# A gated linear attention with a feed-forward block on one core: another written order for its steps, and a normalising weight folded into a centring

## The chip, the core and the metric

The kernel runs on one core of a Trainium2 chip. A core has a matrix engine (TensorE, "PE" in the profile, with its weight loads as "PEld"), a vector engine (VectorE, "DVE"), a scalar engine for functions of one argument (ScalarE, "ACT"), a general engine (GpSimd, "POOL") and queues for transfers between the memory of the chip and the core (mostly SyncE, "SP"). Each engine takes its own instructions in order; engines wait for each other through semaphores. Matrix products land in PSUM, a small memory that VectorE and ScalarE read. The metric is the time of one execution in microseconds of device time.

## The reference

Two blocks, one behind the other. The first is a recurrence with complex decays over 768 positions, for 4 batches of 8 heads of width 48:

```python
mag = np.sqrt(a_re * a_re + a_im * a_im)
scale = np.minimum(mag, 0.999) / (mag + 1e-06)
a_re_n, a_im_n = (a_re * scale, a_im * scale)
for t in range(S):
    S_re, S_im = a_re_n * S_re - a_im_n * S_im + k_t v_t^T, a_re_n * S_im + a_im_n * S_re
    y[:, :, t] = einsum('bhd,bhde->bhe', q[:, :, t], S_re)
```

(The loop is shortened here: the decays act on the rows of the state.) Its output, 3072 rows of 384, enters the second:

```python
h = x @ w_in                                   # 384 -> 1024
sm = softmax(h)
solu = h * sm
ln = (solu - solu.mean()) / np.sqrt(solu.var() + 1e-06) * g_ln
return ln @ w_out                              # 1024 -> 384
```

The weights w_in, w_out and g_ln come to the kernel as float64 for the two matrices, and are converted on the core.

## The kernel before

There are N = 24 **chunks**: 6 stretches of 128 positions, each for 4 batches. Two chunks (two batches of a stretch) form a **group**; there are 12 groups. The function `whole` holds the fast path; `general` is a fallback that runs only if a flag says so, and is not touched.

**Preparation of a group** (`prep_steps`, L648 to L756). It turns the decays of both chunks into running logarithms of magnitude (f_lr) and running phases (f_x, then f_f), in small steps: s0 (clip on VectorE, then a logarithm and an inverse on ScalarE), s1 (four VectorE passes to the tangent of the half angle; the last two become a step of their own by the change), square, s2 and fourth (ScalarE), s3 and s4 (magnitude), totals (L691: a product with a triangular matrix on TensorE that sums the logarithms, then a VectorE clamp that writes f_lr), angle (L725: arctangent on ScalarE, then a VectorE pass that adds what the previous stretch handed on, f_on), phases (L733: a product on TensorE, f_phase, then ScalarE and VectorE passes), trig (L746: sine and cosine into f_cs), decay (L698: two exponentials), decayed (L706: k and q multiplied by them, one call for each chunk), ends (L711: the decay of the whole chunk, turned by a small TensorE transpose, f_tot). The arctangent and the sine need another table set on ScalarE than exponential and logarithm; to_trig and to_exp load one, and each pair of chunks needs both.

**Then a chunk.** doubled (L764) multiplies k and q by cosine and sine into f_k2 and f_q2 (the profile calls them f_k and f_q, with L768), turn (L775) transposes them on TensorE in four calls (k and q, two halves each) and ScalarE copies each result out of PSUM. score (L790) multiplies them in two halves and VectorE applies the causal mask (f_att), values (L802) forms the output of the chunk from f_att and the carried state, VectorE copies it out (f_xn), and carry (L818) updates the state (f_d, f_state).

**Then the feed-forward block of that chunk** (`ffn_steps`, L835): turn_x (f_xt, f_xT), up (L847, f_h) and solu (L854: exponential on ScalarE, product on VectorE, f_z) in two halves, turn_z (L861, f_zt, f_zT) in two halves, norm (L870: statistics on VectorE, two tiny GpSimd instructions, f_rs), down (L888, f_o) in two halves, and store (L895: scaled copy f_ot on VectorE, then the transfer to the output).

The order is written out by hand for TensorE, VectorE and ScalarE: each executes in the order in which `whole` calls the steps. The steps of three stages are laid side by side in the loop over n (L989 on): chunk n goes through score, values and carry; chunk n-1 through turn_x, up, solu, turn_z and norm; chunk n-2 through down, and n-3 through store. In an even step n the group after (`now`) goes from s1 to phases; in an odd one through trig, decay, decayed and ends, while `then`, the group behind it, does s0. Chunk n+1 is doubled and turned during step n.

The tiles sit in rings of few buffers, and a step waits until the reader of the buffer's previous user is through. The ring ps_t in PSUM has two places, which f_xt, f_turned, f_L, f_phase, f_zt and f_tot use in the order in which they are called; f_o has one place, f_score and f_h two each. The raw weights (f_raw) have six places for fourteen tiles (six of w_in, eight of w_out); fetch transfers one tile, raised (ScalarE) and convert (VectorE) turn it into float32. They are transferred a second time from step 4 on, only to be looked at by inspect.

Before the loop stands the **head**: the preparation of group 0, woven with the conversion of w_in. Steps n = 0 and 1 of the loop also convert w_out: for each of its eight tiles raised (ScalarE), convert (VectorE), scale (L634, ScalarE: w_out times g_ln); after n = 1's come centre (L637: a product with ones gives the column means, then eight VectorE passes subtract them).

Of the kernel before, what the change touches and what calls it, by code (L numbers as in the profile page):

```python
# [10 lines left out]
FP = mybir.dt.float32  # L11
# [3 lines left out]
AF = mybir.ActivationFunctionType  # L15
# [3 lines left out]
P = 128  # L19
# [497 lines left out]
def whole(ctx, tc, flag, q, k, v, a_re, a_im, moe_w_in, moe_w_out, moe_g_ln, out):  # L517
# [76 lines left out]
    def weight_steps():  # L594


        NW = 512
        steps = []
        for w, src, nk in ((w_in, moe_w_in, KD), (w_out, moe_w_out, KF)):
            wide = src.bitcast(I32).rearrange("(c p) w -> p c w", p=P)  # L600
            nf = w.shape[2]
            for f0 in range(0, nf, NW):
                for c in range(nk):
                    steps.append((w, wide, c, f0, min(NW, nf - f0)))

        def fetch(i):
            w, wide, c, f0, n = steps[i]
            raw = rawp.tile([P, NW, 2], I32, tag="raw", name="f_raw")[:, 0:n]
            nc.sync.dma_start(out=raw.rearrange("p n u -> p (n u)"), in_=wide[:, c, 2 * f0:2 * (f0 + n)])
            T["raw", i] = raw  # L610

        def raised(i):

            w, wide, c, f0, n = steps[i]
            y = T["bits", i] = bits.tile([P, NW], I32, tag="bits", name="f_bits")[:, 0:n]
            nc.scalar.activation(out=y.bitcast(FP), in_=T["raw", i][:, :, 0].bitcast(U32), func=AF.Identity,
                                 scale=2.0 ** -29, bias=magic)
            nc.scalar.activation(out=y, in_=y.bitcast(FP), func=AF.Identity, bias=mmagic)

        def convert(i):  # L620
            w, wide, c, f0, n = steps[i]
            hi, x = T["raw", i][:, :, 1], w[:, c, f0:f0 + n].bitcast(I32)

            nc.vector.tensor_scalar(out=x, in0=hi, scalar1=3, scalar2=0x3FFFFFFF, op0=OP.logical_shift_left,
                                    op1=OP.bitwise_and)
            nc.vector.scalar_tensor_tensor(out=x, in0=hi, scalar=-2 ** 30, in1=x, op0=OP.bitwise_and,
                                           op1=OP.bitwise_or)
            nc.vector.tensor_tensor(out=x, in0=x, in1=T["bits", i], op=OP.add)

        def inspect(i):  # L630
            nc.vector.tensor_reduce(out=least[:, i:i + 1], in_=T["raw", i][:, :, 1].bitcast(FP), axis=AX.X, op=OP.min,
                                    apply_absolute_value=True)

        def scale(c):  # L634
            nc.scalar.activation(out=w_out[:, c], in_=w_out[:, c], func=AF.Copy, scale=g_ln[:, c:c + 1])

        def centre():  # L637
            ps = ps_o.tile([P, DM], FP, tag="o", padded_shape=[P, 512], name="f_mean")
            for c in range(KF):
                nc.tensor.matmul(out=ps, lhsT=ones, rhs=w_out[:, c], start=(c == 0), stop=(c == KF - 1))  # L640
            for c in range(KF):
# [3 lines left out]
        return fetch, raised, convert, inspect, scale, centre  # L645


    def prep_steps(g):  # L648
# [3 lines left out]
        def s0():  # L652
            for nm in ("lr", "x0", "u"):
# [5 lines left out]
            nc.scalar.activation(out=lr, in_=ar, func=AF.Ln)  # L659
            nc.scalar.activation(out=x0, in_=lr, func=AF.Exp, scale=-1.0)  # L660
            nc.vector.tensor_scalar(out=ai, in0=ai, scalar1=1e15, scalar2=-1e15, op0=OP.min, op1=OP.max)

        def s1():

            ar, ai, x0 = st["ar"], st["ai"], st["x0"]
            nc.vector.tensor_tensor(out=ai, in0=ai, in1=x0, op=OP.mult)
            nc.vector.tensor_tensor(out=x0, in0=ar, in1=x0, op=OP.mult)
            nc.vector.scalar_tensor_tensor(out=x0, in0=x0, scalar=2.0, in1=ai, op0=OP.subtract, op1=OP.mult)
            nc.vector.tensor_scalar(out=x0, in0=x0, scalar1=1.5, scalar2=-1.5, op0=OP.min, op1=OP.max)  # L669

# [40 lines left out]
        def ends():  # L711
# [6 lines left out]
            e2 = sml.tile([GH, 2, D], FP, tag="e2", name="f_e2")  # L718
            nc.vector.tensor_copy(out=e2, in_=e.unsqueeze(1).to_broadcast([GH, 2, D]))
            ps = ps_t.tile([P, GH], FP, tag="t", padded_shape=[P, 512], name="f_tot")  # L720
            nc.tensor.transpose(out=ps[0:D2], in_=e2.rearrange("p u d -> p (u d)"), identity=ident[0:GH, 0:GH])
            tot = T["tot", g] = sml.tile([D2, GH], FP, tag="tot", name="f_tot")
# [2 lines left out]
        def angle():  # L725
            x0 = st["x0"]
            nc.scalar.activation(out=x0, in_=x0, func=AF.Arctan)  # L727
            if ti > 0:

                nc.vector.scalar_tensor_tensor(out=x0[0:1], in0=T["on", g - B // GB], scalar=2.0 * math.pi,  # L730
                                               in1=x0[0:1], op0=OP.mult, op1=OP.add)
# [14 lines left out]
        def trig():  # L746
# [8 lines left out]
        return dict(s0=s0, s1=s1, square=square, s2=s2, fourth=fourth, s3=s3, s4=s4, totals=totals, decay=decay,  # L755
                    decayed=decayed, ends=ends, angle=angle, phases=phases, trig=trig)  # L756

    def to_trig():
        nc.scalar.preload_act_table_set("trig_and_small")
# [180 lines left out]
    nc.vector.memset(magic, MAGIC)  # L940
    nc.vector.memset(mmagic, -MAGIC)
    nc.vector.memset(seen, 0.0)
    fetch, raised, convert, inspect, scale, centre = weight_steps()
    fetch(0)
    fetch(1)
    load(0, ("k", "q"))
# [6 lines left out]
    prep = [prep_steps(g) for g in range(NG)]  # L953
    first = prep[0]
    first["s0"]()
    to_trig()
    first["s1"]()
    raised(0)
    first["square"]()
    first["angle"]()  # L960
    convert(0)
    to_exp()
    first["s2"]()
    raised(1)
    first["s3"]()
    first["phases"]()
    convert(1)
    first["s4"]()
    first["totals"]()
    raised(2)  # L970
    convert(2)
    first["fourth"]()
    first["decay"]()
    to_trig()
    first["trig"]()
    to_exp()
    first["decayed"](0)
# [6 lines left out]
    raised(3)  # L984
    convert(3)
    prep[1]["s0"]()

    last = {}
    for n in range(N + 2):  # L989
# [8 lines left out]
        turn_x, up, solu, turn_z, norm = last[n - 1][:5] if n - 1 in range(N) else 5 * (None,)  # L998
# [7 lines left out]
        if n == 0:  # L1006
            for i in range(6, 14):
                fetch(i)
        if 4 <= n < 18:
            fetch(n - 4)  # L1010

        if n - 3 in range(N):
            last.pop(n - 3)[6]()
        if turn_x:
            turn_x()
        if n < N:
            score(0)
            score(1)
        if now and not odd:
            now["s1"]()  # L1020
        if now and odd:
            now["trig"]()
            to_exp()
            now["decay"]()
        if down:
            down(0)
        if nxt and not odd:
            doubled(nxt)
        if n == 0:
            raised(4)  # L1030
            convert(4)
        if n < N:
            values()
        if now and not odd:
            now["square"]()
        if up:
            up(0)
            solu(0)
        if now and not odd:
            now["s2"]()  # L1040
        if now and odd:
            now["decayed"](0)
        if nxt and odd:
            doubled(nxt)
        if now and odd:
            now["decayed"](1)
        if nxt:
            turn("k", nxt, 0)
            turn("q", nxt, 0)
        if n == 0:  # L1050
            raised(5)
            convert(5)
        if up:
            up(1)
            solu(1)
        if now and not odd:
            now["s3"]()
        if now and odd:
            now["ends"]()
# [5 lines left out]
        if n in (0, 1):  # L1065
            for i in range(6 + 4 * n, 10 + 4 * n):
                raised(i)
                convert(i)
                scale(i - 6)
        if n == 1:  # L1070
            centre()
        if now and not odd:
            now["s4"]()
        if then and odd:
            then["s0"]()
        if up:
            turn_z(0)
        if now and not odd:
            now["totals"]()
            now["fourth"]()  # L1080
            to_trig()
            now["angle"]()
        if down:
            down(1)
        if up:
            turn_z(1)
            norm()
        if 4 <= n < 18:
            inspect(n - 4)
        if n == N:  # L1090
            verdict()
        if now and not odd:
            now["phases"]()
    last.pop(N - 1)[6]()


@with_exitstack
# [54 lines left out]
```

## Time and profile before

| What | Value |
|---|---|
| Median of three runs | 688.5 us (687.51 to 689.68) |
| The profiled execution | 690.01 us |
| Its span, first to last instruction | 688.1 us |
| Mean granted clock of TensorE | 0.896 of full speed |
| Transfers | 42.23 MB, mean 61 GB/s |

The page also gives the span in 40 slices of 17.2 us, in tenths of busy time:

```profile
PE   1162776878878878878878878878878888789995
...
PEclk9975775999999999988999999999997999899999
DMA  8978150203214214214214203203203000000000
```

The first seven slices are the head with n = 0 and 1; TensorE is little used there, its granted clock (PEclk) is low in several of them, and the transfers are dense until the fourth. From there to slice 36 stand the pairs of steps. Time of the profile is that of one execution, and its rows are given as start and length in microseconds from the first instruction; in brackets stands how long the engine was idle before, and what released it.

### The profile page before, as it was taken

The page shows a single profiled execution, that of the slowest core. Times are in us where ns is not written, and L with a number is a line of the kernel's source. Part 1 is how long each engine was busy: PE and PEld are TensorE (multiplying, and loading weights), DVE is VectorE, ACT ScalarE, POOL GpSimd, SP SyncE. Part 2 cuts the span into 40 slices and gives each one's busy share as a digit, 9 for nine tenths or more (in the row PEclk, how much of TensorE's full clock was granted, in tenths as well). Part 3 has the DMA queues.
Part 4 walks back from the last instruction along what each step waited for, and adds up shares of the span by engine and source line. Part 5 has one row for each costly group of instructions (what it writes and reads, how often), then busy time and mean ns, then how long its engine had stood idle before and what let it go on. Part 6 is the DMA issues. An engine that isn't in the chain of part 4 may idle for free. (4 is left out here: it accounts for less than half of the span.)

```text
span 688.1 us, 13068 instructions
## 1 busy us (share of the span) xinstructions
PE 530.5 (77%) x5604; PEld 332.2 (48%) x5604; DVE 374.9 (54%) x713; ACT 312.5 (45%) x507; POOL 18.1 (3%) x52
## 2 busy tenths in 40 slices
PE   1162776878878878878878878878878888789995
PEld 0042434545445445445445545545545455446653
DVE  4585546455556556555556556566564556454322
ACT  5667542642643543542543543543643453542221
POOL 0000000000000000000000000000000000000000
PEclk9975775999999999988999999999997999899999
DMA  8978150203214214214214203203203000000000
GB/s 209 219 181 227 21 142 30 47 13 81 48 36 104 48 36 105 47 39 100 47 37 104 47 14 81 47 14 81 47 13 82 1 13 14 1 13 13 13 12 29
DMA packets 134243, 42.23 MB, mean 61 GB/s; under 512 B 127392, under 2 KB 130464, under 8 KB 134176
## 3 DMA queue, kind: packets, MB, share of 16 engines
q1 hardware_dynamic: 133328, 40.91, 25.4%
q8 instruction: 46, 0.75, 0.5%
q10 hardware_dynamic: 848, 0.40, 0.2%
q14 instruction: 21, 0.17, 0.1%
HBM read 36.51 MB, written 4.72 MB: 60 GB/s over the span
## 5 line engine op out<-in xcount | busy, mean ns | idle before, releaser
L850 PE MATMUL f_h<-f_w_in,f_xT 128*128 128x512 f32 x288 | 144.9, 644 | 0.0
L892 PE MATMUL f_o<-f_w_out,f_zT 128*128 128x384 f32 x384 | 134.7, 494 | 1.0 <-DVE f_ot L897 1.0
L859 DVE TENSOR_TENSOR f_z<-f_h,f_z 128x512 f32<-128x512 f32 x48 | 33.2, 692 | 141.3 <-ACT f_z L858 141.3
L892 PEld LDWEIGHTS f_o<-f_w_out,f_zT 128*128 128x128 f32 x384 | 73.4, 199 | 46.7 <-issue 8.2
L858 ACT ACTIVATE f_z<-f_h 128x512 f32<-128x512 f32 x48 | 28.7, 597 | 121.7 <-PE f_h L850 121.7
L850 PEld LDWEIGHTS f_h<-f_w_in,f_xT 128*128 128x128 f32 x288 | 56.6, 211 | 55.0 <-issue 53.1
L780 PE MATMUL f_turned<-f_mats,f_k 128*96 128x128 f32 x192 | 38.0, 332 | 47.0 <-DVE f_k L768 47.0
L867 PE MATMUL f_zt<-f_mats,f_z 128*128 128x128 f32 x192 | 35.5, 317 | 33.5 <-ACT f_kT L782 33.5
L782 ACT COPY f_kT<-f_turned 96x512 f32<-96x512 f32 x48 | 27.5, 574 | 70.3 <-PE f_turned L780 70.3
L780 PEld LDWEIGHTS f_turned<-f_mats,f_k 128*96 128x96 f32 x192 | 24.1, 148 | 67.0 <-DVE f_k L768 57.4
L797 PE MATMUL f_score<-f_qT,f_kT 96*128 96x128 f32 x384 | 49.3, 284 | 0.0
L867 PEld LDWEIGHTS f_zt<-f_mats,f_z 128*128 128x128 f32 x192 | 26.0, 160 | 47.7 <-ACT f_kT L782 38.7
L695 PE MATMUL f_L<-f_lr,f_mats 128*128 128x384 f32 x48 | 33.0, 842 | 19.7 <-DVE f_lr L688 19.7
L868 ACT COPY f_zT<-f_zt 128x512 f32<-128x512 f32 x48 | 27.7, 582 | 44.8 <-PE f_zt L867 44.8
L797 PEld LDWEIGHTS f_score<-f_qT,f_kT 96*128 96x128 f32 x384 | 47.1, 200 | 0.0
L799 DVE TENSOR_TENSOR f_att<-f_score,f_mats 128x512 f32<-128x512 f32 x48 | 32.7, 688 | 17.1 <-PE f_score L797 17.1
L809 PEld LDWEIGHTS f_y<-f_v,f_att 128*32 128x32 f32 x1536 | 30.8, 110 | 14.7 <-issue 11.4
L780 PE MATMUL f_turned<-f_mats,f_q 128*96 128x128 f32 x192 | 37.1, 328 | 0.1
L809 PE MATMUL f_y<-f_v,f_att 128*32 128x48 f32 x1536 | 34.6, 209 | 2.2 <-DVE f_att L799 2.2
L672 ACT ACTIVATE f_ar<-f_x 128x768 f32<-128x768 f32 x12 | 10.1, 843 | 57.3 <-DVE f_x L669 57.3
L815 DVE COPY f_xn<-f_y 128x384 f32<-128x384 f32 x24 | 13.3, 554 | 39.6 <-PE f_y L812 36.2
L740 PE MATMUL f_phase<-f_x,f_mats 128*128 128x384 f32 x48 | 22.2, 554 | 14.5 <-ACT f_x L727 14.2
(98 smaller groups left out, 753.9 us busy)
## 6 DMA issues: line engine op xcount, KB each, us to landing
f_raw<-in_moe_w_in_dram SPq DMA_DIRECT2D x12, 512.0 KB, 5.1
f_raw<-in_moe_w_out_dram SPq DMA_DIRECT2D x16, 384.0 KB, 3.4
f_ar<-in_a_re_dram SPq DMA_DIRECT2D x24, 192.0 KB, 3.5
f_ai<-in_a_im_dram SPq DMA_DIRECT2D x24, 192.0 KB, 3.4
f_q<-in_q_dram SPq DMA_DIRECT2D x24, 192.0 KB, 3.7
f_k<-in_k_dram SPq DMA_DIRECT2D x24, 192.0 KB, 3.7
f_v<-in_v_dram SPq DMA_DIRECT2D x24, 192.0 KB, 3.4
out_dram<-f_ot SPq DMA_DIRECT2D x24, 192.0 KB, 2.3
```

The lines of the kernel that those rows point to most:

```text
L695: nc.tensor.matmul(out=ps, lhsT=tri, rhs=lm, start=True, stop=True)
L780: nc.tensor.transpose(out=ps[0:D2, i], in_=T[nm + "2", c][:, half * 4 + i].rearrange("p u d -> p (u d)"), identity=ident)
L782: nc.scalar.copy(out=T[nm + "T", c][:, half * 512:half * 512 + 512], in_=ps[0:D2].rearrange("p i t -> p (i t)"))
L797: nc.tensor.matmul(out=ps[:, i], lhsT=KT[:, x * P:(x + 1) * P], rhs=QT[:, x * P:(x + 1) * P], start=True, stop=True)
L799: nc.vector.tensor_tensor(out=st["att"][:, half * 4:half * 4 + 4], in0=ps, in1=tri.unsqueeze(1).to_broadcast([P, 4, P]), op=OP.mult)
L809: nc.tensor.matmul(out=y[r:r + 32, hs], lhsT=st["att"][:, x, r:r + 32], rhs=V[:, hs], start=True, stop=(ti == 0))
L850: nc.tensor.matmul(out=h, lhsT=st["xT"][:, c * P:(c + 1) * P], rhs=w_in[:, c, half * 512:(half + 1) * 512], start=(c == 0), stop=(c == KD ...
L858: nc.scalar.activation(out=z, in_=h, func=AF.Exp, accum_out=sums[:, ti * B + b, half:half + 1])
L859: nc.vector.tensor_tensor(out=z, in0=h, in1=z, op=OP.mult)
L867: nc.tensor.transpose(out=ps[:, i * P:(i + 1) * P], in_=st["z"][:, c * P:(c + 1) * P], identity=ident)
L868: nc.scalar.copy(out=st["zT"][:, half * 512:(half + 1) * 512], in_=ps)
L892: nc.tensor.matmul(out=st["o"], lhsT=st["zT"][:, c * P:(c + 1) * P], rhs=w_out[:, c], start=(c == 0), stop=(c == KF - 1))
```

## The change

The loop now begins at n = 2; what n = 0 and 1 did is written out ahead of it, together with a new head. g_ln is no longer multiplied into w_out by ScalarE. Instead the mean is formed from the unscaled w_out, with g_ln/1024 as the other factor of the product (one column of it repeated 128 times as weights), in two portions of four tiles, and the centring pass computes w_out times g_ln minus the mean:

```diff
-        def scale(c):
-            nc.scalar.activation(out=w_out[:, c], in_=w_out[:, c], func=AF.Copy, scale=g_ln[:, c:c + 1])
+        def mean(c):
+            if c == 0:
+                gs = T["gs"] = const.tile([P, KF], FP, name="f_gs")
+                nc.vector.tensor_scalar(out=gs, in0=g_ln, scalar1=1.0 / FF, scalar2=None, op0=OP.mult)
+                T["mean"] = ps_o.tile([P, DM], FP, tag="o", padded_shape=[P, 512], name="f_mean")
+            nc.tensor.matmul(out=T["mean"], lhsT=T["gs"][:, c:c + 1].to_broadcast([P, P]), rhs=w_out[:, c],
+                             start=(c == 0), stop=(c == KF - 1))
...
-                nc.tensor.matmul(out=ps, lhsT=ones, rhs=w_out[:, c], start=(c == 0), stop=(c == KF - 1))
...
-                nc.vector.scalar_tensor_tensor(out=w_out[:, c], in0=ps, scalar=-1.0 / FF, in1=w_out[:, c],
-                                               op0=OP.mult, op1=OP.add)
+                nc.vector.scalar_tensor_tensor(out=w_out[:, c], in0=w_out[:, c], scalar=g_ln[:, c:c + 1],
+                                               in1=T["mean"], op0=OP.mult, op1=OP.subtract)
```

Four steps are cut in two so that their parts can be placed apart: s0 gives up its two ScalarE passes (inverse), s1 its last two VectorE passes (tangent), ends its transpose and copy (tots), angle its VectorE pass (on). The order of the calls in the loop, before and after (in brackets the chunk, where it isn't plain):

| Even step, before | Even step, after |
|---|---|
| store(n-3), turn_x, score 0 and 1 | score 0 and 1, turn_x |
| s1 | square, s2 |
| down 0, doubled(n+1) | doubled(n+1), down 0, tots, s3 |
| values, square, up 0, solu 0, s2 | values, up 0, solu 0, s4 |
| turn k and q (first halves), up 1, solu 1, s3 | turn k and q (first halves), norm(n-2), up 1, solu 1, inspect |
| carry, turn k and q (second halves), s4 | carry, turn k and q (second halves), fourth, to_trig, angle |
| turn_z 0, totals, fourth, to_trig, angle, down 1 | down 1, totals, on, store(n-2) |
| turn_z 1, norm(n-1), inspect, phases | turn_z 0 and 1, phases |

| Odd step, before | Odd step, after |
|---|---|
| store(n-3), turn_x, score 0 and 1 | score 0 and 1, turn_x |
| trig, to_exp, decay, down 0, values | trig, to_exp, decay, down 0, values |
| up 0, solu 0, decayed 0, doubled(n+1), decayed 1 | decayed 0, doubled(n+1), up 0, solu 0, decayed 1, s0 of the group behind |
| turn k and q (first halves), up 1, solu 1, ends | turn k and q (first halves), norm(n-2), up 1, solu 1, inspect |
| carry, turn k and q (second halves), s0 of the group behind | carry, turn k and q (second halves), ends, inverse and s1 of the group behind |
| turn_z 0, down 1, turn_z 1, norm(n-1), inspect | down 1, store(n-2), tangent of the group behind, turn_z 0 and 1 |

In the part that is written out, the transfers of the last eight weight tiles are called ahead of those of group 1's k, q and v and group 2's decays (before: behind them). The head does all of group 0's logarithms and exponentials before its arctangent and sines, so that it has three table loads instead of five. Group 1's preparation and chunk 0 and 1 are woven with the eight conversions of w_out, and s0, inverse, s1 and tangent of group 2 stand ahead of n = 2:

```diff
+    score, values, carry = chunk_steps(1)
+    last[0] = ffn_steps(0)
+    turn_x, up, solu, turn_z = last[0][:4]
+    turn_x()
+    score(0)
+    score(1)
+    second["fourth"]()
+    second["s4"]()
+    raised(8)
+    up(0)
+    values()
+    solu(0)
+    second["totals"]()
+    convert(8)
...
+    for c in range(4, 8):
+        mean(c)
+    third["s0"]()
+    third["inverse"]()
+    centre()
+    third["s1"]()
+    third["tangent"]()
+
+    for n in range(2, N + 2):
```

More of the change, by code (lines that the diff above doesn't have):

```diff
@@ L942, in whole @@
     nc.vector.memset(seen, 0.0)
-    fetch, raised, convert, inspect, scale, centre = weight_steps()
+    fetch, raised, convert, inspect, mean, centre = weight_steps()
     fetch(0)
@@ L983, in whole, with both @@
     first["ends"]()
-    raised(3)
-    convert(3)
-    prep[1]["s0"]()
-    last = {}
-    for n in range(N + 2):
+    first["tots"]()
+    def both(nm, c):
+        return [lambda: turn(nm, c, 0), lambda: turn(nm, c, 1)]
+    for i in range(6, 14):
+        fetch(i)
+    load(1, ("k", "q", "v"))
+    load(2, ("ar", "ai"))
+    last = {}
+    second, third = prep[1], prep[2]
+    score, values, carry = chunk_steps(0)
+    score(0)
+    score(1)
+    second["s0"]()
+    second["inverse"]()
+    raised(5)
+    values()
+    doubled(1)
+    convert(5)
+    turn("k", 1, 0)
+    turn("q", 1, 0)
+    carry()
+    second["s1"]()
+    turn("k", 1, 1)
+    turn("q", 1, 1)
+    second["tangent"]()
+    second["square"]()
+    second["s2"]()
+    raised(6)
+    convert(6)
+    second["s3"]()
+    raised(7)
+    convert(7)
+    score, values, carry = chunk_steps(1)
+    last[0] = ffn_steps(0)
+    turn_x, up, solu, turn_z = last[0][:4]
+    turn_x()
+    score(0)
+    score(1)
+    second["fourth"]()
+    second["s4"]()
+    raised(8)
+    up(0)
+    values()
+    solu(0)
+    second["totals"]()
+    convert(8)
+    up(1)
+    solu(1)
+    to_trig()
+    second["angle"]()
+    carry()
+    raised(9)
+    convert(9)
+    for c in range(4):
+        mean(c)
+    second["phases"]()
+    second["trig"]()
+    to_exp()
+    second["decay"]()
+    raised(10)
+    convert(10)
+    second["decayed"](0)
+    doubled(2)
+    raised(11)
+    convert(11)
+    for half in range(2):
+        for nm in ("k", "q"):
+            turn(nm, 2, half)
+    second["decayed"](1)
+    second["ends"]()
+    raised(12)
+    convert(12)
+    turn_z(0)
+    turn_z(1)
+    raised(13)
+    convert(13)
+    for c in range(4, 8):
+        mean(c)
+    third["s0"]()
[4 more added lines that the diff above has]
+    for n in range(2, N + 2):
         g, odd = divmod(n, GB)
@@ L1018, in whole @@
             score(1)
-        if now and not odd:
-            now["s1"]()
+        if turn_x:
+            turn_x()
         if now and odd:
@@ L1044, in whole @@
             doubled(nxt)
+        if up:
+            up(0)
+            solu(0)
         if now and odd:
             now["decayed"](1)
+        if then and odd:
+            then["s0"]()
+        if now and not odd:
+            now["s4"]()
         if nxt:
@@ L1055, in whole @@
             solu(1)
[L1056 to L1059, printed above, removed]
+        if 4 <= n < 18:
+            inspect(n - 4)
         if n < N:
@@ L1082, in whole @@
             now["angle"]()
+        if now and odd:
+            now["ends"]()
+        if then and odd:
+            then["inverse"]()
+            then["s1"]()
         if down:
             down(1)
+        if now and not odd:
+            now["totals"]()
+            now["on"]()
+        if down:
+            last.pop(n - 2)[6]()
+        if then and odd:
+            then["tangent"]()
         if up:
+            turn_z(0)
             turn_z(1)
-            norm()
-        if 4 <= n < 18:
-            inspect(n - 4)
         if n == N:
```

97 lines of the change are left out of this document (41 added, 56 removed).

## The prediction

> **What bounds the kernel now.** I read the page's busy times first, then the list of waits, then TensorE's own order of time through one pair of steps.
>
> ```profile
> span 688.1 us, 13068 instructions
> ...
> PE 530.5 (77%) x5604; PEld 332.2 (48%) x5604; DVE 374.9 (54%) x713; ACT 312.5 (45%) x507; POOL 18.1 (3%) x52
> ```
> ```profile
> POOL f_s L885 <- DVE f_s L884: 654.8, 24, 112.0
> ...
> PE f_turned L780 <- DVE f_k L768: 47.0, 13, 6.9
> PE f_zt L867 <- ACT f_kT L782: 33.5, 19, 4.0
> ...
> PE f_tot L721 <- DVE f_e L719: 18.2, 9, 2.0
> ```
>
> TensorE (PE) is the busiest engine, and the waits that matter are its own: GpSimd's 654.8 is an engine with nothing to do. Three of PE's waits recur through the run: the turning of k, the turning of z, and the small f_tot. The next rows show them in one pair (n = 10 and 11), with the marks of some steps around it. Each step n starts at its f_xt.
>
> ```profile
> 112.56 0.90 PE L842 MATMUL f_xt<-f_mats,f_xn 128*128 128x128 f32 x3 [5.28 <-ACT f_zT L868]
> ...
> 120.99 2.84 PE L850 MATMUL f_h<-f_w_in,f_xT 128*128 128x512 f32 x6
> ...
> 165.55 0.49 PE L842 MATMUL f_xt<-f_mats,f_xn 128*128 128x128 f32 x3
> ...
> 334.97 0.88 PE L824 MATMUL f_d<-f_v,f_k 128*32 128x48 f32 x48
> ...
> 339.87 0.86 PE L867 MATMUL f_zt<-f_mats,f_z 128*128 128x128 f32 x4 [3.01 <-ACT f_kT L782]
> ...
> 348.87 1.95 PE L797 MATMUL f_score<-f_qT,f_kT 96*128 96x128 f32 x16
> 350.65 2.75 PE L892 MATMUL f_o<-f_w_out,f_zT 128*128 128x384 f32 x8
> 353.33 0.29 PE L809 MATMUL f_y<-f_v,f_att 128*32 128x48 f32 x8
> ...
> 354.86 2.84 PE L850 MATMUL f_h<-f_w_in,f_xT 128*128 128x512 f32 x6
> 361.00 1.09 PE L780 MATMUL f_turned<-f_mats,f_k 128*96 128x128 f32 x4 [3.30 <-DVE f_k L768]
> ...
> 368.21 0.19 PE L721 MATMUL f_tot<-f_mats,f_e 16*96 16x16 f32 x1 [2.02 <-DVE f_e L719]
> ...
> 630.04 0.49 PE L842 MATMUL f_xt<-f_mats,f_xn 128*128 128x128 f32 x3
> ...
> 647.41 0.49 PE L842 MATMUL f_xt<-f_mats,f_xn 128*128 128x128 f32 x3
> ```
>
> Steps n = 4 to 21 take 630.04 - 165.55 = 464.49 us, 51.61 us a pair. Step n = 22 has no preparation of a later group in it and takes only 647.41 - 630.04 = 17.37 us, almost without gaps. So the packed work of a pair can be worked out: two such steps 34.7, two carries (f_d, 0.81 from the row at 334.97 to the next group) 1.6, and four 128x384 products of the preparation. A 128x384 matmul is two records; eight records take 353.33 - 350.65 = 2.68, so four products take 2.7. Less some 0.6 of small gaps left in step 22, that is 38.4 us. The other 13.2 us of a pair are gaps and a slow clock:
>
> ```profile
> 322.43:373.97 51.54, 42.62 (x506) 26.84 (x505) 30.03 (x57) 23.86 (x39) 1.15 (x4) 0.93 0.26 62
> ```
> ```profile
> 362.00:366.00 4.00, 4.00 (x11) 2.03 (x10) 0.75 (x2) 1.16 (x2) 0.00 (x0) 0.74 0.65 127
> 366.00:370.00 4.00, 1.98 (x58) 1.69 (x57) 1.95 (x7) 0.87 (x3) 0.00 (x0) 1.00 0.35 70
> ```
> ```profile
> 632.00:636.00 4.00, 4.00 (x117) 2.66 (x120) 2.58 (x4) 0.00 (x0) 0.00 (x0) 1.00 0.00 0
> ```
>
> These are windows: length, then busy time of PE, weight loads, VectorE, ScalarE, GpSimd, then PE's granted clock. PE is busy 42.62 of 51.54, so 8.9 idle; 42.62 - 38.4 = 4.2 is work done at a lower clock, granted behind the long gaps (0.74 after the 3.30, while the 2.02 gap lies in a window at 1.00). VectorE (DVE) has 30.0 us of work in the pair and ScalarE (ACT) 23.9, so neither forbids 38.4. What remains is whether the new order lets them hand over in time.
>
> **The steady pair, odd step.** The rows of DVE and ACT say why k is late.
>
> ```profile
> 349.80 0.94 ACT L749 ACTIVATE f_cs<-f_cs,f_bias 128x768 f32<-128x768 f32 x1 [0.25 <-DVE f_cs L743]
> ...
> 353.53 0.83 ACT L702 ACTIVATE f_ar<-f_lr 128x768 f32<-128x768 f32 x1
> ```
> ```profile
> 354.99 0.56 DVE L815 COPY f_xn<-f_y 128x384 f32<-128x384 f32 x1 [3.45 <-PE f_y L812]
> 358.45 0.69 DVE L859 TENSOR_TENSOR f_z<-f_h,f_z 128x512 f32<-128x512 f32 x1 [2.90 <-ACT f_z L858]
> ...
> 360.00 0.95 DVE L768 TENSOR_TENSOR f_k<-f_cs,f_k 128x768 f32<-128x768 f32 x1
> 360.86 0.95 DVE L768 TENSOR_TENSOR f_q<-f_cs,f_q 128x768 f32<-128x768 f32 x1
> ```
>
> DVE copies f_xn and then stands 2.90 us, because solu(0) is written ahead of decayed(0) and doubled, and its exponential waits for PE's up(0). The change writes those two ahead of up(0) and solu(0). I lay the new order out with T = 0 at the score. Score 1.8 and f_xt 0.3 (now behind the score), down(0) 2.7 and values 1.5 end at 6.3. ACT's f_xT copy now stands in front of the trigonometry, so that its 4.6 us (349.80 to 354.36) run from 2.8 to 7.4. DVE copies f_xn until 6.95, multiplies the two decayed halves (360.00 - 358.45 less the z product, 0.94) until about 7.9, and k is doubled at 8.8, q at 9.7. PE leaves up(0) at 9.1. So k's turn waits for nothing and q's about 0.3: **the 3.3 us gap goes**, and with it the slow clock behind it.
>
> ```profile
> 325.35 0.95 DVE L666 TENSOR_TENSOR f_ai<-f_ai,f_x 128x768 f32<-128x768 f32 x1
> ...
> 328.32 0.56 DVE L669 TENSOR_SCALAR f_x<-f_x 128x768 f32<-128x768 f32 x1
> ```
> ```profile
> 366.94 0.69 DVE L859 TENSOR_TENSOR f_z<-f_h,f_z 128x512 f32<-128x512 f32 x1 [4.19 <-ACT f_z L858]
> ...
> 373.80 0.62 DVE L897 TENSOR_SCALAR f_ot<-f_o,f_rs 128x384 f32<-128x384 f32 x1
> ```
>
> Moved into this step are inverse, s1 and tangent of the group after (DVE 3.44, from 325.35 to 328.8, formerly in the even step). They come behind s0, norm, z, inspect, carry and ends, which took 6.3 without their waits (366.94 to 374.3, some 15 instructions), and around the store. From f_xn on DVE has 3.2 + 0.6 + 0.9 + 6.3 + 3.4 = 14.4 us in a row, to 21.0. PE's own work in an odd step is half of the pair's without the four products of the preparation, (38.4 - 2.7)/2 = 17.9, and it is through at 18.2. Nothing of PE waits for the tail of DVE in this step (turn_z needs only z, finished near 15). The f_tot transpose moves into the next even step behind down(0), where its input is long there: the 2.02 goes. norm, one step later in its chunk's life, has its result ready some 4 us before the store; GpSimd's two small instructions fit there.
>
> **Even step.** It starts with DVE 2.8 late. The masks of score are done at 4.1; values come at 4.9 behind score, f_xt and down(0) (the store, placed ahead of tangent, frees f_o's only buffer at 1.3, before down(0) asks at 2.1). The cover is thus 0.8 us. fourth and angle now run on ACT under down(1), and both f_zt behind totals, so **the 3.01 gap** (f_zt waiting for a copy behind s3's two ScalarE passes) **goes**. New waits come in its place: the turning buffer has two places, used by totals, turn_z and phases in turn.
>
> ```profile
> 342.14 0.56 DVE L696 TENSOR_SCALAR f_lr<-f_L 128x384 f32<-128x384 f32 x1 [1.80 <-PE f_L L695]
> ...
> 344.37 0.95 DVE L730 SCALAR_TENSOR_TENSOR f_x<-f_on,f_x 1x768 f32<-1x768 f32 x1 [0.39 <-ACT f_x L727]
> ```
>
> Each f_zt waits for one f_lr pass (0.56, mostly under the matmul before), and phases for f_on's 0.95 behind both: 0.1 + 0.2 + 0.4 by my layout, bounded by 0 and 2.0 (all three passes in the open). So pair = 38.4 + 0.3 + 0.7 = 39.4, and I add 0.8 for handovers of 0.03 to 0.1 us that I did not sum: **40.2**, between 38.4 and 43.
>
> Does the slow clock go wholly? If it shrank only with the idle time, 4.2 x 1.8/8.9 = 0.8 us a pair would stay, 8 us over the run. But the window behind the 2.02 us gap has the full clock and the one behind 3.30 has not, so short gaps seem to cost none of it, and I take nothing. The Trainium skill ("TensorE: Matmul & The Clock Gate", section "Why this matters for your kernels") says the same of long gaps only: matmul bursts should have no idle gap of more than about 3 us between them, or the clock falls to half. By that rule the term is nothing too, against 8 us by the proportion; the two windows agree with the rule.
>
> **The head.** Up to n = 2 the change removes the eight scalings.
>
> ```profile
> 94.08 0.64 ACT L616 ACTIVATE f_bits<-f_raw,f_bias 128x384 f32<-128x384 uint32 x1
> ...
> 96.52 0.63 ACT L616 ACTIVATE f_bits<-f_raw,f_bias 128x384 f32<-128x384 uint32 x1
> ```
> ```profile
> L762 ACT ACT_TABLE_LOAD x14 | 18.0, 1283 | 0.9 <-PEq L1136 0.7
> ...
> L635 ACT ACTIVATE f_w_out<-f_w_out,f_g_ln 128x384 f32<-128x384 f32 x8 | 4.9, 616 | 5.0 <-DVE f_w_out L628 5.0
> ```
>
> Each tile of w_out cost ACT 2.44 us (94.08 to 96.52), of which half is the scaling and the wait for DVE ahead of it: 4.9 + 5.0 = 9.9 us for eight, in two serial blocks through which PE had next to nothing. centre keeps eight DVE passes of equal size; the mean's matmuls keep their number, and one tiny DVE pass is new. A weight load that repeats one column is not in this trace; between free and the double of a plain load (0.5 us each at half clock) it stays within 8 us, under the conversions, and I take it as plain. Two of the head's five table loads go, 1.28 us each; as angle and two more conversions now stand ahead of the first doubling, I count nothing for them. third's tangent now precedes n = 2 and leaves its middle, which cancels by the end of values. The transfers of w_out are written ahead of group 1's k, q, v. The last of these wait for convert(7); their consumers stand more than 20 us behind it, against landings of 3 to 5 us. So the head, measured to the end of values in n = 2 (120.99), gains 9.9; the bounds are 0 (another chain is as long) and 22 (PE packed from 93 on).
>
> **Sum.** Profiled execution 690.0 (span 688.1, 1.9 around it). Head -9.9. Rest of n = 2 and 3: 165.55 - 120.99 = 44.6 against 40.2 - 6.4 = 33.8, -10.8. Nine pairs: 9 x (51.61 - 40.2) = -102.7. The tail from n = 22 stays. 690.0 - 123.4 = 566.6; the median of before is 1.5 below its profiled run, so **565 us**.
>
> **Rivals.**
> 1. Slower: the clock. Denser work might be granted less. With clock c a pair costs 38.4/c + 1.8; with 9.86 pairs' worth at stake the gain is gone at 52.7 a pair, c = 0.754. At 0.74, the window at 362, it is 53.7: about 698 us. For it: the mean clock of the pair is 0.93 now, for whatever reason. Against it: 632 to 636 is fully busy at 1.00. Chance 0.05.
> 2. DVE becomes late. The cover of the masks is 0.8 us; if tangent ends 3 us later than I lay it, PE waits 2.2 a pair, 587 us, more if the clock falls as well. For it: DVE has 14.4 us in a row. Chance 0.12.
> 3. The order does not do what it says for k: the f_xT copy now delays the decays, and if ACT is 2 us later than 7.4, the turn still waits about 2: 42 a pair, 583 us. Chance 0.10.
> 4. More than I count: head -20 and pairs of 39: 543 to 554 us. Chance 0.09.
>
> My forecast, 555 to 582, has 0.62; no change 0.02. A difference within 0.3% is what a measurement of this kernel could not tell from none. Faster 0.62 + 0.12 + 0.10 + 0.09 = 0.93, same 0.02, slower 0.05. The range 550 to 592 takes in the forecast, rival 3, most of 2 and half of 4.
>
> **What would show it.** PE's wait for f_turned <- f_k falls below 10 us, f_zt <- f_kT and f_tot vanish, the clock row reads 9 from n = 2 on, pairs come every 40 us, values of n = 2 end near 111, and PE's share of the span is near 90%. A wait f_y <- f_att would show rival 2, f_turned <- f_k of 2 us each rival 3, a clock below 0.9 without gaps rival 1. I am wrong if DVE's or ACT's chain takes more than PE's 40 us a pair.

## The result and the profile after

The changed kernel takes 554.65 us (median of four runs, 554.25 to 555.96) against 688.8 us for the kernel before: ratio 0.8057, 95% interval 0.8038 to 0.8076. The forecast was 565 us in a range of 550 to 592. The profiled execution has a span of 553.1 us, 135.0 less than before. The page's busy times and two of its rows in 40 slices (13.8 us each now) answer to those shown of before:

```profile
span 553.1 us, 13053 instructions
...
PE 482.6 (87%) x5604; PEld 309.4 (56%) x5604; DVE 367.3 (66%) x714; ACT 305.4 (55%) x497; POOL 17.9 (3%) x52
...
PE   0265744799999999999999999999999999999994
...
PEclk9957786899999999999999999999999999999999
```

TensorE has the same 5604 matmul records, but they are busy for 482.6 us in place of 530.5: the difference is for the most part matmuls that no longer run at a lower clock. From slice 9 to the last but one both rows read 9 without a break. The other digits below 9 are the head, which now holds nearly all that is left to gain.

The list of waits (engine, line, awaited; then total us, times, longest us):

```profile
PE f_L L703 <- DVE f_lr L696: 18.5, 1, 18.5
PE f_turned L796 <- DVE f_k L784: 17.8, 4, 10.7
PE f_h L866 <- ACT f_xT L861: 7.5, 1, 7.5
...
PE f_phase L756 <- DVE f_x L746: 2.9, 10, 0.3
PE f_turned L796 <- DVE f_q L784: 2.7, 11, 0.3
...
PE f_y L825 <- DVE f_att L815: 0.3, 1, 0.3
```

The waits of before, 47.0 for k, 33.5 for z and 18.2 for f_tot, are gone from the pairs; k's 17.8 stands ahead of them, 17.5 us in three places of the head and 0.3 in n = 3. What the pairs have in their stead is nine of the ten waits of the phases and nine of the eleven of q's turn, about 0.27 us each.

PE's order of time gives the four stretches by which the forecast was summed (a step now starts at its first score):

```profile
109.19 2.84 PE L866 MATMUL f_h<-f_w_in,f_xT 128*128 128x512 f32 x6
...
142.15 1.95 PE L813 MATMUL f_score<-f_qT,f_kT 96*128 96x128 f32 x16
...
496.07 1.95 PE L813 MATMUL f_score<-f_qT,f_kT 96*128 96x128 f32 x16
```

| Stretch | Before, us | After, us | Difference | Forecast |
|---|---|---|---|---|
| Head, to the end of values in n = 2 | 120.99 | 109.19 | -11.8 | -9.9 |
| Rest of n = 2, and n = 3 | 44.56 | 32.96 | -11.6 | -10.8 |
| Nine pairs, n = 4 to 21 | 464.49 | 353.92 | -110.6 | -102.7 |
| n = 22 to the end of the span | 58.06 | 57.03 | -1.0 | 0 |
| Span | 688.1 | 553.1 | -135.0 | -123.4 |

One pair in a window (length, then busy time of PE, weight loads, VectorE, ScalarE, GpSimd, then PE's granted clock):

```profile
142.15:180.90 38.75, 38.23 (x498) 24.60 (x497) 28.63 (x56) 23.63 (x39) 1.48 (x4) 1.00 0.34 69
```

PE is idle for 0.5 us of these 38.75 us, against 8.9 of 51.54 before, and the clock is 1.00 against 0.93. (This window ends a little ahead of the next pair's score; pairs come every 39.55 us.)

### The profile page after: what moved, and what is told of

Read it like the earlier page. It is cut to its first block, busy times and chain, and to the rows that moved or that the text cites. A ratio compares the mean times of both kernels' runs of the same rounds, so it can differ in the third digit from the quotient of the medians.

```text
span 553.1 us, 13053 instructions
## 1 busy us (share of the span) xinstructions
PE 482.6 (87%) x5604; PEld 309.4 (56%) x5604; DVE 367.3 (66%) x714; ACT 305.4 (55%) x497; POOL 17.9 (3%) x52
## 5 line engine op out<-in xcount | busy, mean ns | idle before, releaser
L866 PE MATMUL f_h<-f_w_in,f_xT 128*128 128x512 f32 x288 | 135.7, 609 | 7.5 <-ACT f_xT L861 7.5
L908 PEld LDWEIGHTS f_o<-f_w_out,f_zT 128*128 128x128 f32 x384 | 70.2, 192 | 43.1 <-DVE f_w_out L645 2.7
L866 PEld LDWEIGHTS f_h<-f_w_in,f_xT 128*128 128x128 f32 x288 | 52.0, 193 | 57.7 <-issue 48.0
L796 PE MATMUL f_turned<-f_mats,f_k 128*96 128x128 f32 x192 | 32.1, 293 | 17.8 <-DVE f_k L784 17.8
L798 ACT COPY f_kT<-f_turned 96x512 f32<-96x512 f32 x48 | 27.6, 576 | 18.1 <-PE f_turned L796 18.1
L703 PE MATMUL f_L<-f_lr,f_mats 128*128 128x384 f32 x48 | 19.0, 522 | 18.5 <-DVE f_lr L696 18.5
L796 PE MATMUL f_turned<-f_mats,f_q 128*96 128x128 f32 x192 | 31.3, 289 | 2.7 <-DVE f_q L784 2.7
L896 DVE BATCH_NORM_STATS2 f_bs<-f_z 128x6 f32<-128x512 f32 x48 | 30.7, 680 | 0.0
L704 DVE TENSOR_SCALAR f_lr<-f_L 128x384 f32<-128x384 f32 x24 | 13.3, 556 | 25.8 <-PE f_L L703 25.0
L828 PE MATMUL f_y<-f_state,f_qT 96*32 96x48 f32 x1280 | 29.8, 205 | 0.0
L798 ACT COPY f_qT<-f_turned 96x512 f32<-96x512 f32 x48 | 28.1, 585 | 2.9 <-PE f_turned L796 1.8
```

What stands on the lines that cost most here:

```text
L796: nc.tensor.transpose(out=ps[0:D2, i], in_=T[nm + "2", c][:, half * 4 + i].rearrange("p u d -> p (u d)"), identity=ident)
L798: nc.scalar.copy(out=T[nm + "T", c][:, half * 512:half * 512 + 512], in_=ps[0:D2].rearrange("p i t -> p (i t)"))
L828: nc.tensor.matmul(out=y[r:r + 32, hs], lhsT=T["qT", c][:, x * P + r:x * P + r + 32], rhs=state[b][:, hs], start=False, stop=True)
L866: nc.tensor.matmul(out=h, lhsT=st["xT"][:, c * P:(c + 1) * P], rhs=w_in[:, c, half * 512:(half + 1) * 512], start=(c == 0), stop=(c == KD ...
L896: nc.vector.bn_stats(out=bs[:, i], in_=z[:, i * 512:(i + 1) * 512])
L908: nc.tensor.matmul(out=st["o"], lhsT=st["zT"][:, c * P:(c + 1) * P], rhs=w_out[:, c], start=(c == 0), stop=(c == KF - 1))
```

## Experiments

Each kernel was timed beside the kernel before on the same chip. The medians of the kernel before were 688.1 to 689.8 us there, so a difference of one or two us between two of the runs below is not told from none.

### One half of the odd step's order undone

```diff
-        if now and odd:
-            now["decayed"](0)
-        if nxt and odd:
-            doubled(nxt)
         if up:
             up(0)
             solu(0)
+        if now and odd:
+            now["decayed"](0)
+        if nxt and odd:
+            doubled(nxt)
```

> The changed kernel with decayed(0) and doubled in odd steps put back behind up(0) and solu(0); nothing else. My theory: the turn of k waits again about 3 us in each odd step with preparation and the clock falls behind it, 4.5 to 5.5 us a pair, ten pairs: 600 to 610 us, f_turned <- f_k about 30 us more. Rival: the rest of the new order gives VectorE enough lead that the gap stays under 2 us and costs no clock: 565 to 578 us.

603.86 us, 49.2 more than the changed kernel. The list of waits shows the group of before again, in nine more places than in the changed kernel:

```profile
PE f_turned L796 <- DVE f_k L784: 50.5, 13, 10.7
```

That is 32.7 us more of waiting for 49 us more of time. The rest is the clock, which falls again behind each gap: over the 4 us behind each of the ten waits of 3.31 us it is 0.50 to 0.65. The pairs' odd steps (the last apart) take 23.0 to 23.4 us where the changed kernel's take 18.1. The page's clock row shows it only in part, since a few us at half clock in a slice of 15.1 us can still read 9:

```profile
PEclk9997878997998998998999999999989989989999
```

Two calls in another place, undone alone, thus cost 49 of the 134 us. The theory held, and the rival, that the rest of the order gives enough lead, fell.

### The even step's s3 and s4 back in their old places

```diff
-        if now and not odd:
-            now["s3"]()
         if n < N:
             values()
...
-        if now and not odd:
-            now["s4"]()
         if nxt:
             turn("k", nxt, 0)
...
             up(1)
             solu(1)
+        if now and not odd:
+            now["s3"]()
...
         if now and not odd:
+            now["s4"]()
             now["fourth"]()
```

> The changed kernel with s3 put back behind solu(1) and s4 behind the second turns in even steps. My theory: s3's two ScalarE passes then run ahead of the copies of the second turns; f_L is 1 to 2 us later, the phases 2 to 3 us; a gap just below what costs clock: 2 to 3 us a pair, 573 to 585 us. Rival 1: the 3 us gap of before comes back with the slow clock, 5 us a pair: 600 us or more. Rival 2: the later order of turn_z alone hid it: below 560 us.

577.34 us, 22.7 more. By the marks of f_xt each even step from n = 2 to 18 takes 2.1 us more (23.51 us in place of 21.41 in the pairs), and n = 20 takes 3.2 more. In its list of waits:

```profile
PE f_L L703 <- DVE f_lr L696: 30.0, 11, 18.6
...
PE f_phase L756 <- DVE f_x L746: 9.9, 9, 1.1
```

The magnitude's product comes 1.05 us late in each of these steps and the phases 1.09, two short gaps with the clock at 1.00 behind them. In n = 20 the product is 1.99 us late, and the clock is 0.61 over the 4 us behind it:

```profile
496.44 2.03 PE L703 MATMUL f_L<-f_lr,f_mats 128*128 128x384 f32 x4 [1.99 <-DVE f_lr L696]
```

The theory held in size and in place, that one step's clock apart: the early places of s3 and s4 keep their ScalarE passes off the path, and the old gap of 3 us does not come back. I take it, without a run that tests it, that this is because the copies of the second turns are no longer awaited by turn_z at once.

### How much lead VectorE has: two and four added passes

Passes that write a tile nobody reads, ahead of tangent in the nine odd steps that have one:

```diff
         if then and odd:
+            for _ in range(4):
+                nc.vector.tensor_tensor(out=pad, in0=pad, in1=pad, op=OP.mult)
             then["tangent"]()
```

> The changed kernel with four added VectorE passes of 128x768 (0.87 us each, 3.5 in all) ahead of tangent in the nine odd steps that have one; they write a tile nobody reads. My theory: the masks of the next even step have a cover of 0.8 us, so PE waits 2.0 to 2.7 us for f_att in nine steps, without cost in clock: 573 to 580 us, f_y <- f_att 18 to 25 us. Rival: VectorE makes the lag up elsewhere, below 560 us; other rival: a gap of this size costs clock too, 590 us or more.

586.64 us, 32 more: more than the theory allowed, less than the rival. The wait is as it said, 2.46 us in eight even steps and 2.60 in the last:

```profile
PE f_y L825 <- DVE f_att L815: 22.6, 10, 2.6
```

All but 0.3 of these 22.6 us are new (one wait of 0.3 stands in the head of the changed kernel too). Most of the rest is the clock. Windows of one even step (columns as above; the clock is the number behind GpSimd's count):

```profile
316.00:320.00 4.00, 2.26 (x8) 1.07 (x6) 3.90 (x6) 0.05 (x1) 0.00 (x0) 1.00 0.06 20
320.00:324.00 4.00, 3.28 (x130) 2.60 (x131) 4.00 (x8) 1.80 (x3) 0.00 (x0) 0.72 0.19 39
324.00:328.00 4.00, 4.00 (x15) 2.06 (x14) 0.94 (x2) 3.10 (x6) 0.00 (x0) 0.85 0.86 162
```

The first holds most of the idle time, the other two some 3.4 us at half clock behind it. By the f_xt marks this happens in five of the nine even steps, 1.6 us each: successive pairs take 42.1, 43.7, 43.8 and 42.1 us (143.40, 185.49, 229.18, 272.96, 315.04). 42.1 is the pair of 39.55 and the wait; the others pay the clock besides. With two passes:

> The changed kernel with two added VectorE passes (1.74 us) ahead of tangent in the nine odd steps. With four of them the wait for f_att was 2.6 us in a step and the clock fell behind it in some steps, not in all. My theory: the wait is 0.9 us a step here and no step loses clock: 562 to 564 us, clock row 1.00 in the pairs. Rival: any gap can cost clock, in proportion: 567 us or more.

559.92 us, 5.3 more, 0.6 a step; the list of waits has 4.7 us in ten waits for f_att, and the clock is 1.00 through all pairs. My figure of 0.9 a step was too high, and the traces say why. With four passes:

```profile
313.25 1.95 PE L813 MATMUL f_score<-f_qT,f_kT 96*128 96x128 f32 x16
...
319.98 1.28 DVE L815 TENSOR_TENSOR f_att<-f_score,f_mats 128x512 f32<-128x512 f32 x2
...
320.72 0.29 PE L825 MATMUL f_y<-f_v,f_att 128*32 128x48 f32 x8 [2.46 <-DVE f_att L815]
```

The two masks run until 321.26, but values starts at 320.72, when the first is done: it begins with the first half of the heads. In the changed kernel the first mask (0.68 us from 342.77) ends 1.4 us ahead of values (344.84), and this is the lead. The masks start 2.87 us behind the score there, 4.75 with two passes and 6.73 with four, so they are 1.88 and 3.86 us later, and the waits of 0.47 and 2.46 us leave 1.4 both times. The cover of 0.8 us counted to the end of the second mask. That no step lost clock with two passes is as expected.

### The folding alone, in two forms

In the kernel before, scale is dropped and the mean formed with the share of g_ln. In the first form all eight products stand where they were in centre, and the share is formed just ahead of them:

> The kernel before with g_ln folded into the centring and nothing else; all calls stay where they were. My theory: in the two serial blocks a tile of w_out costs ScalarE 1.3 us instead of 2.44, about 1.1 x 8 = 9 us off the head, none in the pairs: 679 to 682 us. Rival: the scalings lay beside other work, and the head of the changed kernel is shorter because of its weaving: 685 us or more.

689.9 us, ratio 1.0008 (0.9987 to 1.003): nothing. The order of time says where the gain went. VectorE forms the share behind the last conversion, and all products wait for it:

```profile
98.68 0.17 DVE L637 TENSOR_SCALAR f_gs<-f_g_ln 128x8 f32<-128x8 f32 x1
98.90 7.52 PE L639 MATMUL f_mean<-f_w_out,f_gs 128*128 128x384 f32 x16 [7.21 <-DVE f_gs L637]
...
106.46 4.29 DVE L644 SCALAR_TENSOR_TENSOR f_w_out<-f_w_out,f_g_ln,f_mean 128x384 f32<-128x384 f32 x8 [7.62 <-PE f_mean L639]
```

The conversions end near 98.7 us, 5 earlier than before (the last scaling there is done near 103.9), but the products then run in one stretch, 7.5 us at a mean clock of 0.72, and centre starts at 106.46; before it was 105.61. In the second form the share is formed early in n = 0 and each product stands behind its conversion:

```diff
         for i in range(6 + 4 * n, 10 + 4 * n):
             raised(i)
             convert(i)
-            scale(i - 6)
+            mean(i - 6)
```

> The kernel before with the folding alone, this time with the share g_ln/1024 formed early in n = 0 and each mean product right behind its conversion, so that neither stands behind the last conversion as in the first try. My theory now: the conversions end some 5 us earlier and so do the products; centre starts near 99 us in place of 105.6, 682 to 684 us. Rival: the old head is bound elsewhere at this place and the folding is worth nothing in either form: 688 us or more.

681.98 us against 688.47 us beside it, ratio 0.9919 (0.9889 to 0.9949): 6 us, if the products are placed for it. Centre starts at 98.00 in the profiled execution. Of the eleven executions nine took 680.2 to 683.2 us and two 688.4 and 688.6; what sets these two apart was not looked into.

### The folding taken out of the changed kernel

```diff
     raised(6)
     convert(6)
+    scale(0)
...
     raised(13)
     convert(13)
+    scale(7)
```

The mean is formed with ones and centred as before.

> The changed kernel with the scaling by g_ln put back on ScalarE, one call behind each of the eight conversions, and the mean with ones again. My theory: each scaling and the wait for VectorE in front of it is back on ScalarE's path, 8 x 1.2 = 10 us: 562 to 566 us. Rival: in the woven head it is covered: below 558 us.

555.95 us, 1.3 more than the changed kernel, and the intervals of the two ratios overlap (0.8053 to 0.8105 here, 0.8038 to 0.8076 there). The rival is right: in the woven head the scalings are covered, and the folding is worth nothing there that these runs can tell from none.

### The new loop behind the old head

> The old head with the old n = 0 and 1 and the scaling, then the new order from n = 2 on. My theory: the steady order alone gives n = 2, 3 and the nine pairs, 11 + 111 us: 565 to 570 us, pairs of 39.5 us. Rival: the new order needs the new head's lead (s1, tangent done early), and without it the pairs drift: pairs above 41 us, 580 us or more.

561.6 us, 7 more than the changed kernel. Its pairs take 39.55 us too, so the steady order carries itself, whatever comes ahead. Its values of n = 2 end at 116.77, where the kernel before has 120.99: 4.2 us of the head's gain belong to the new loop's first step. One reason is that the scores now stand ahead of f_xt and run while that waits for the copies of z (3.05 us still to wait, against 5.28 before):

```profile
109.90 0.90 PE L856 MATMUL f_xt<-f_mats,f_xn 128*128 128x128 f32 x3 [3.05 <-ACT f_zT L882]
...
116.77 1.55 PE L864 MATMUL f_h<-f_w_in,f_xT 128*128 128x512 f32 x3
```

The other 7.6 us to 109.19 are the new head with the folding in it. (The first step has s1 and tangent of group 2 ahead of it here too.)

### What binds the new head

Around 70 us of the changed kernel (all engines, by time) the angle of group 1 is ready on ScalarE at 71.5, but PE has mean products in front of the phases, which wait for a conversion and then run at a mean clock of 0.61 (73.38 to 77.71):

```profile
70.63 0.84 ACT L740 ACTIVATE f_x<-f_x 128x768 f32<-128x768 f32 x1
...
73.38 4.49 PE L640 MATMUL f_mean<-f_w_out,f_gs 128*128 128x384 f32 x8 [3.97 <-DVE f_gs L638]
77.71 1.45 PE L756 MATMUL f_phase<-f_x,f_mats 128*128 128x384 f32 x4
...
84.72 0.83 ACT L710 ACTIVATE f_ar<-f_lr 128x768 f32<-128x768 f32 x1
```

```diff
-    for c in range(4):
-        mean(c)
     second["phases"]()
     second["trig"]()
     to_exp()
     second["decay"]()
+    for c in range(4):
+        mean(c)
```

> The changed kernel with the first four mean products moved from in front of group 1's phases to behind its decays. My theory: in the head PE holds the phases back by 6 us (the products wait for a conversion at 73.4 and run at half clock until 77.7, while the angle is ready at 71.5), and the chain behind them, trig, decay, doubled, is what n = 2 waits for: 548 to 551 us. Rival: the conversions of w_out set the end of the head, no change: 554 to 555 us.

548.73 us, 5.9 less than the changed kernel. In the profiles it is 5.1, and the first score of n = 2 already comes 4.8 us earlier (94.16 in place of 98.96). Nothing else was moved, so it is the chain of group 1 that sets the head's end here; the last conversions stand behind it and come earlier with it. The next kernel follows that (the lines are shown at their new places only): chunk 1's f_xt and scores ahead of the seventh tile's conversion, up(1) behind the phases, conversions in ScalarE's gaps, s1 and tangent of group 2 behind the first scores of n = 2:

```diff
+    turn_x()
+    score(0)
+    score(1)
     raised(6)
     convert(6)
+    up(0)
     second["s3"]()
+    values()
     raised(7)
     convert(7)
...
     second["phases"]()
+    up(1)
+    raised(9)
     second["trig"]()
     to_exp()
+    convert(9)
     second["decay"]()
+    solu(1)
+    for c in range(4):
+        mean(c)
```

> The changed kernel with another order in the head alone (and s1 and tangent of group 2 behind the first scores of n = 2): chunk 1's turn_x and scores ahead of the conversion of the seventh tile, its up(1) behind group 1's phases, the mean products behind group 1's decays, conversions in ScalarE's gaps. My theory: the chain angle, phases, trig, decay, doubled of group 1 sets the start of n = 2, and this order brings its decays from 85.5 to about 75 us: 542 to 547 us with the pairs unchanged at 39.5 us. Rival: behind means_later the conversions of w_out bind, no gain over it: 548 us or more.

543.91 us (542.97 to 545.72), ratio to the kernel before 0.7913 (95% interval 0.7894 to 0.7933). It is 10.7 us faster than the changed kernel, and 4.8 faster than with the products moved alone. Its decays of group 1 end 12.8 us earlier than the changed kernel's, and PE reaches up(0) of n = 2 at 97.45 in place of 109.19:

```profile
71.95 0.83 ACT L710 ACTIVATE f_ar<-f_lr 128x768 f32<-128x768 f32 x1
```

It is the fastest of all kernels run here.

## Why the prediction was right, and where not

**The steady pair: right by its steps.** The layout of the odd step said that k's turn waits for nothing and q's for about 0.3 us; the profile has 2.7 us in eleven waits for q. It placed the copy of f_xn, the doubled k and the doubled q at 6.95, 8.8 and 9.7 us behind the score. VectorE's rows (score at 321.76):

```profile
328.22 0.56 DVE L831 COPY f_xn<-f_y 128x384 f32<-128x384 f32 x1 [3.29 <-PE f_y L828]
...
329.63 0.95 DVE L784 TENSOR_TENSOR f_k<-f_cs,f_k 128x768 f32<-128x768 f32 x1
330.50 0.95 DVE L784 TENSOR_TENSOR f_q<-f_cs,f_q 128x768 f32<-128x768 f32 x1
```

They end 7.0, 8.8 and 9.7 behind it. For the even step the layout said that the masks end at 4.1 and values starts at 4.9; in the profile (score at 339.90) they end at 4.15 and it starts near 4.9:

```profile
339.02 1.04 PE L883 MATMUL f_zt<-f_mats,f_z 128*128 128x128 f32 x8
339.90 1.95 PE L813 MATMUL f_score<-f_qT,f_kT 96*128 96x128 f32 x16
...
358.36 1.30 PE L883 MATMUL f_zt<-f_mats,f_z 128*128 128x128 f32 x8
359.95 1.53 PE L756 MATMUL f_phase<-f_x,f_mats 128*128 128x384 f32 x4 [0.29 <-DVE f_x L746]
```
```profile
342.77 1.28 DVE L815 TENSOR_TENSOR f_att<-f_score,f_mats 128x512 f32<-128x512 f32 x2
```

The ring of two places was allowed 0.7 us a pair. The list of waits shows only the 0.29 in front of the phases, but by the starts the whole is there: from f_zt to what follows it are 1.59 us in the even step and 0.88 in the odd one, 0.71 more. q's turn starts 0.39 us later behind k's in the odd step than in the even one (330.77 to 331.60, 349.04 to 349.48). Less these two the pair of 39.55 is 38.45, the packed work that the layout began with.

**The term that was mis-sized** is the 0.8 us a pair added "for handovers of 0.03 to 0.1 us that I did not sum". The layout itself gave 39.4, the pairs take 39.55, and the last before n = 22 is shorter by 2. The distances from start to start, from which the layout was made, held the handovers already. Over nine pairs this and the short last pair are 7.9 of the 11.6 us by which the sum fell short; 0.8 are in n = 2 and 3, 1.0 in the tail, and 1.9 in the head.

**The slow clock goes wholly:** right for this kernel, which is at 1.00 in each pair. But the reason, that short gaps cost none of it, was read from one gap of 2.02 us, and the same trace of before speaks against it. From n = 3 on that gap stands there eight times; behind six of them the clock is 1.00, and behind two, at 315.47 and 523.67, it is 0.60 and 0.61:

```profile
315.47 0.19 PE L721 MATMUL f_tot<-f_mats,f_e 16*96 16x16 f32 x1 [2.02 <-DVE f_e L719]
```
```profile
315.47:319.47 4.00, 4.00 (x62) 3.53 (x63) 3.06 (x7) 1.64 (x3) 0.00 (x0) 0.60 0.49 96
368.21:372.21 4.00, 3.76 (x65) 2.92 (x66) 3.08 (x7) 1.93 (x4) 0.00 (x0) 1.00 0.46 92
```

The term of nothing came true because the new order leaves no gap above 0.3 us in a pair, not because gaps of 2 us are free. The Trainium skill ("TensorE: Matmul & The Clock Gate", section "Why this matters for your kernels") sets the limit at about 3 us; in these runs gaps of 2.46, 2.02 and 1.99 us cost clock in some places, and gaps of about 1.1 us or less in the pairs never did.

**The head: the size nearly right by luck, the step wrong.** The step was that the eight scalings' 9.9 us of ScalarE come off the head. The head gains 11.8, but the folding gives nothing where the products stand behind the last conversion, 6 us at best in the old head, and nothing clear of the noise in the new one. What shortens the head is the order: 4.2 us from the loop's first step, and most of 7.6 us from the weaving. I had priced the one removed instruction by its wait and not asked what is late next: in the new head it is group 1's chain through angle, phases and decay, as the run with the mean products moved shows. My remark that the products of the mean are under the conversions was wrong as well: in the new head they hold up the phases for 6 us. The sign named for it, f_turned <- f_k below 10 us, was not met either: 17.5 us of that wait stand in the head.

**The rivals.** A lower clock under dense work did not appear: 1.00 with PE 99% busy. VectorE is not late, and its lead of 1.4 us was measured by the added passes: 2.5 us of wait in nine steps cost 32 us with the clock, where the rival was priced at 22 and more if the clock fell. k's turn not saved: fell, by both the profile and the run that undid it.

**Left open:** what share of the remaining gain of the pair (12.1 us, of which the odd step's two calls carry 5.0 and s3 with s4 2.1 when undone) belongs to norm, tots and the store; these were not moved one by one. In the head, the other order of the transfers and the two table loads fewer were not tried alone.

## What to carry to other kernels

When one engine carries the work and the others hand over to it in a written order, lay the new order out from start-to-start distances of the old trace: here that gave the pair to 0.2 us. A call that waits for the bound engine (an exponential of its product) belongs behind the calls that the bound engine itself will need next. And do not price a removed instruction by its own time and wait alone: find the chain that ends last without it, or the gain stays on paper, as the folding's did.

## What the runs showed of the hardware that was not expected

A gap well below 3 us can cost TensorE its clock, and the same gap does so in one place and not in the next. The clock here is the mean over the 4 us behind the gap; where it is not low it reads 1.00:

| Gap, us | Run | Places | With a low clock behind |
|---|---|---|---|
| 3.0 to 4.0 | before, from 130 us on | 20 | 20 (0.50 to 0.65) |
| 2.60 | four added passes | 1 | 0 |
| 2.46 | four added passes | 8 | 5 (0.58 to 0.70) |
| 2.02 | before, from n = 3 on | 8 | 2 (0.60, 0.61) |
| 1.99 | s3 and s4 back | 1 | 1 (0.61) |
| 1.04 to 1.10 | s3 and s4 back | 18 | 0 |

With four passes the step lost about 1.6 us where the clock fell (pairs of 43.7 us) and nothing where it did not (42.1 us). The two windows of 4 us shown there, at 0.72 and 0.85, lack 1.1 and 0.6 us of full clock, which is some 3.4 us at half clock. The Trainium skill ("TensorE: Matmul & The Clock Gate", "Part 1") says that activity is judged in free-running windows of about 3.4 us; the trace agrees with that length, and gaps that meet such a window in different places would explain the two kinds of places, which no run here tested further. A gap shorter than a whole window was enough.
